# First modulation weights loaded and multiplied by halves of their columns, key-weight chunks loaded between them, one late subtraction, new instruction orders

## The chip, the core and the metric

The kernel runs on one core of a Trainium2 chip. Its five queues are TensorE (PE, with PEld for its weight loads), VectorE (DVE), ScalarE (ACT), GpSimd (POOL) and SyncE (SP), which issues most DMAs. The metric is device time in microseconds of one execution. The kernel before took 1062.74 us, the median of 3 runs (1060.46 to 1064.73).

## What is computed

An adaLN block on 2048 tokens of width D = 576: a linear attention with 32 heads of 18, then an MLP of 4608, both modulated by a condition c. Cut to what matters:

```python
mod = (silu(c) @ w_mod).reshape(1, 6, 1, -1)          # c: (1, 576), w_mod: (576, 3456)
sa, ca, ga, sb, cb, gb = (mod[:, i] for i in range(6))
h = layernorm(x) * (1 + ca) + sa
x = x + ga * attention(h, A_wqkv, A_wo)                # phi(k)^T v, phi(q) kv / (phi(q) z)
h = layernorm(x) * (1 + cb) + sb
return x + gb * (silu(h @ B_w1) @ B_w2)
```

The first thing that the kernel needs is sa and ca: the first 1152 columns of w_mod, multiplied by silu(c).

## The kernel before

**Tiling.** Tokens lie in tiles of 128, four to a block. The width 576 is four chunks of 128 (k = 0 to 3) and a tail of 64 (k = 4, `KC`), stacked twice where a high and a low part are needed. Products in the attention are split into a high part in a reduced f32 and the rest ("hi" and "lo"), so a chunk of a projection is three products.

**The start, in program order.** SP loads x tiles 0 and 1 (L437), the tail rows of w_mod (`tmod`, L468, two loads), the four chunks of w_mod's first 1152 columns (`mods`, L460, 576 KB each), the key weights' chunks (`acc[0]` to `acc[4]`, L404 to L407), x tiles 2 and 3, and the query weights' chunks. VectorE sets `ones` (L552), a 128 x 128 tile, and some small constants; GpSimd makes the identity `ident`. `keep_busy(n)` (L539) puts n matmuls of `ones` by `ones` on TensorE whose result nobody reads. TensorE then transposes c (L560), ScalarE makes silu(c), `sc` (L561). Two layer norms (statistics L347, pow on GpSimd L353) give x tiles 0 and 1, transposed by `turn_tiles` (L531).

**The modulation.** VectorE multiplies `mods[0]` by `sc` (L583) and adds `mods[1]` and `mods[2]` times theirs (L586), each on 1152 columns at once; of `mods[3]` (`last`) it adds the second plane (L593). TensorE sums over partitions with one-column matmuls, `mod_col_of` (L522): for each k one of `mods[0]`'s first plane, one of `last`'s first plane by `sc`, one of the second plane; `tail_cols` (L519) adds the tail rows. `add_cols` (L526) takes the sums out of PSUM as shift and scale. With these, ScalarE (L607) and VectorE (L372, L272) turn each transposed chunk into hT's hi and lo part. The key weights are split on ScalarE (`w_hi`, L477) and VectorE or GpSimd (`w_lo`, L482, L484). `first_k` and `k_part` (L548) are the key projections of x tiles 0 and 1, 56 matmuls. L873 are the projections after that, L1269 the transposes of tiles 2 and 3.

**The end.** The last unit of the MLP (`up_steps` with `last`) makes four values f00, f01, f10, f11 (L1965 to L1971) and splits them into hi and lo operands hp0, hb0, hp1, hb1: "<" is the copy on ScalarE (L2005), ">" the subtraction on VectorE (L2009). `plain_steps` then multiplies them with w2 for eight token tiles (L2065), the first four with hp0 and hb0, the last four with hp1 and hb1, and stores.

**What sets the order.** `arrange` (L262) chains each engine's instructions in the order that `ORDERS` lists by number. Numbers count an engine's instructions in the order in which the program emits them, from `begun`. So each queue is in order, by these lists, and an instruction that waits holds all behind it. TensorE's numbers at the start: 0 to 10 fillers, 11 the transpose of c, 12 to 19 fillers, 20 to 24 `tail_cols`, 25 to 34 `turn_tiles`. VectorE's: 0 `ones`, 1 to 5 small memsets, 6 and 7 the halves of x tile 0's statistics, 9 and 10 those of tile 1. GpSimd's: 0 and 1 the identity, 2 the first pow.

Of the kernel before, what the change touches and what calls it, by code (L numbers as in the profile page):

```python
# [24 lines left out]
def kernel(ctx: ExitStack, tc, A_x, A_wqkv, A_wo, B_x, B_w1, B_w2, c, w_mod, out):  # L25
# [33 lines left out]
    def behind(instructions):  # L59

        with ExitStack() as order:
# [7 lines left out]
            0-24 27-29 25-26 30-44 47 49 51 53 55 57-58 45-46 48 50 59-62 52 54 63-66 69-70 56 73-74 67-68 71-72 75-76  # L69
            79-80 83-84 87-88 77-78 91-92 81-82 85-86 101-102 89-90 95-96 99-100 93-94 103 97-98 106-107 104-105  # L70
            108-123 128-133 136-137 124-127 134 138-139 135 140-163 166-169 164-165 170-187 306 188-191 330 307
            194-201 192-193 202-211 331 212-219 308-309 332-335 220-233 310-311 336-337 234-243 250-255 244-245
            256-265 246-249 312-319 266-267 338-339 278-281 340-343 282-287 344-345 288-295 320-329 268-269 346-347
            270-273 296-297 274-277 354-367 298-301 348-349 368-369 350-351 302-303 352-353 370-381 304-305 382-385
            402-403 386-395 404-409 418-419 410-411 396-397 446-447 420-421 412-417 448-455 398-399 456-457 422-427
            400-401 428-445 458-471 474-475 472-473 476-497 502-507 498-501 508-525 586-591 526-529 610-611 530-533
            592-593 534-535 612-613 536-537 594-595 614-617 538-541 558-561 618-623 542-543 596-597 624-625 598-599
            626-629 562-563 544-549 600-603 564-565 604-607 630-631 550-551 566-569 632-633 608-609 570-573 552-557
            634-641 658-663 642-657 664-665 574-583 666-667 584-585 682-695 668-675 726-727 676-677 728-729 698-701
            696-697 702-703 678-681 704-713 730-731 714-725 732-751 754-757 752-753 758-773 782-787 774-777 788-793  # L80
            778-781 794-803 890-891 804-809 892-893 866-867 894-895 868-869 810-811 870-873 812-815 896-897 816-829
            874-875 898-903 830-843 876-885 904-907 844-851 908-909 886-889 852-855 910-911 856-863 914-917 912-913
            918-919 864-865 920-929 938-951 930-937 1006-1011 952-953 978-979 962-973 1012-1015 954-955 980-997
            1016-1017 998-1005 1018-1035 956-959 1036-1051 1062-1069 974-975 1052-1055 976-977 960-961 1056-1061
            1070-1073 1147-1158 1074-1081 1090-1091 1082-1089 1092-1099 1159 1100-1105 1118-1135 1106-1109 1160-1166
            1136-1139 1110-1111 1140-1141 1167-1170 1112-1113 1142-1143 1114-1117 1144-1145 1207-1222 1197-1200
            1195-1196 1201 1223-1226 1146 1227-1230 1171-1194 1255-1256 1297-1298 1257-1262 1231-1254 1202-1203
            1263-1266 1204-1206 1267-1270 1299-1302 1271 1303-1304 1272-1295 1305-1324 1296 1325-1382 1399-1402
            1383-1386 1427-1428 1403-1408 1429-1434 1387-1392 1435-1440 1393-1398 1409-1414 1441-1444 1415-1422
            1455-1456 1423-1424 1445-1452 1425-1426 1453-1454 1457-1476 1483-1484 1511-1514 1485-1492 1515-1516  # L90
            1477-1482 1493-1496 1517-1534 1497-1504 1535-1538 1505-1510 1539-1552 1567-1568 1553-1558 1595-1596
            1559-1562 1569-1572 1563-1566 1597-1600 1573-1580 1601-1602 1581-1586 1603-1606 1587-1594 1639-1642 1623
            1607-1622 1627 1643-1646 1624-1625 1671-1672 1647-1648 1626 1649-1658 1628 1699-1700 1659-1662 1629
            1673-1674 1630 1663-1666 1675-1676 1631 1701 1632-1633 1635-1637 1634 1702-1710 1638 1711-1714 1677-1680
            1755-1756 1715-1716 1681-1682 1717-1722 1667 1683-1684 1668 1723-1726 1669-1670 1685-1698 1727 1741
# [12 lines left out]
            2138-2140 2157-2160 2141-2142 2161-2164 2175-2178 2165-2174 2183-2185 2193-2194 2203-2204 2195 2186 2205
            2179-2180 2196 2189-2190 2181-2182 2191 2206 2192 2187 2207-2208 2188 2209-2214 2199 2197-2198 2215-2216
            2200-2202 2217-2218 2227 2221-2222 2239 2228-2230 2223-2226 2231 2253 2240 2232-2233 2241-2244 2254-2257  # L110
            2245 2234 2219 2246-2248 2235 2258 2220 2249-2252 2236-2238 2259-2267 2273 2268 2279-2281 2269-2271 2274
            2282 2272 2285 2275-2278 2286-2290 2283-2284 2297 2291 2298-2314 2292-2296 2315-2356 2365-2366 2377
            2357-2358 2378-2381 2359-2362 2367 2382 2371 2363-2364 2389-2390 2368 2372-2374 2369 2375-2376 2370
            2391-2400 2407-2412 2383 2413-2414 2384-2388 2447-2449 2427-2428 2450-2451 2429-2431 2401-2402 2452
            2415-2416 2403 2432 2417 2404 2433 2405 2418 2434 2419-2420 2406 2499 2511-2516 2465-2472 2421-2424 2435
            2485 2500 2425-2426 2436-2439 2486 2440 2487-2491 2441-2442 2492 2443-2444 2501-2504 2445-2446 2453-2458
            2537 2523-2528 2473-2478 2459-2464 2538-2544 2493 2479 2494-2498 2529-2530 2480-2484 2505-2510 2551-2556
            2517-2521 2563-2567 2522 2568-2570 2531-2536 2577-2584 2557-2559 2545-2550 2591-2596 2571-2576 2560
            2603-2604 2561-2562 2605-2608 2597-2599 2585-2587 2600-2602 2588-2590 2615-2621 2609-2612 2623-2624 2622
            2625 2613-2614 2626 2629-2636 2627-2628 2637-2642 2683-2687 2649 2663 2650 2643-2646 2664 2647-2648  # L120
            2651-2654 2688 2655 2665-2668 2656-2662 2669-2675 2689-2690 2677-2679 2676 2680 2691 2681 2692-2695 2682
            2701-2704 2696-2697 2705-2706 2698-2700 2707-2717 2719 2727-2728 2720-2725 2718 2729-2731 2739-2740 2817
            2741-2743 2818 2744-2746 2732-2738 2747-2752 2759-2760 2819-2821 2753-2756 2726 2757 2765-2766 2758
            2761-2762 2767-2770 2763-2764 2771-2776 2785-2787 2835-2836 2777-2778 2837-2838 2805 2779-2781 2839 2782
            2797 2840 2798 2783-2784 2806-2808 2799-2800 2809-2810 2788-2789 2811 2801-2804 2812 2822 2813-2816
            2790-2792 2873-2874 2853 2793 2841 2794-2796 2842-2843 2875-2876 2854-2856 2823-2828 2877-2878 2844 2829
            2879-2880 2845-2846 2830-2833 2857-2859 2847-2848 2834 2893-2897 2849-2850 2861-2865 2860 2866-2867 2898
            2868-2870 2851-2852 2911-2912 2871-2872 2913-2914 2881-2882 2915 2883 2916-2918 2884-2887 2899-2906
            2888-2892 2907-2909 2931-2934 2919-2921 2910 2922-2930
# [472 lines left out]
    for k in START:  # L602
# [7 lines left out]
        if k < KC:  # L610
            first_k(k)
# [1823 lines left out]
```

## Time and profile before

| | |
|---|---|
| median of 3 runs | 1062.74 us |
| the profiled execution | 1062.19 us |
| its span, first to last instruction | 1060.5 us |
| busy: PE, PEld | 1048.6 us (99%), 740.5 us (70%) |
| busy: DVE, ACT, POOL | 867.0 us (82%), 718.5 us (68%), 741.8 us (70%) |
| DMA | 198.75 MB, 187 GB/s over the span |
| granted TensorE clock | 1.00 |

A line of the timeline is: start, length, engine, line of the kernel, operation, the tile written and the tiles read, partitions x elements, count, and in brackets the idle time before it with what ended it. A line of the waits is: who waited for whom, total, times, longest. A window line gives the stretch, its length, the busy time (and instructions) of each engine asked for, the granted clock, the DMA engines' mean busy share and GB/s. Busy TensorE includes the fillers.

### The profile page before, as it was taken

To read this page: it belongs to the slowest core of one execution; us is meant where nothing else is said; L and a number is where in the kernel's file an instruction comes from. 1 tells how busy PE (TensorE), PEld (TensorE's weight loads), DVE (VectorE), ACT (ScalarE), POOL (GpSimd) and SP (SyncE) were. 2 spreads that over 40 slices of the span, in tenths; PEclk is the share of its full clock that TensorE was granted. 3 is DMA by queue.
4 is the path that set the end of the run, shared out by engine and by line. 5 is a ranking of instruction groups with operands and counts; after the bars stand their busy time and mean duration, and the time that the engine had idled before them with its cause. 6 is when DMAs were issued, how large, how long until landed. Compare 5 with 4: busy or idle time off the path is not lost.

```text
span 1060.5 us, 19049 instructions
## 1 busy us (share of the span) xinstructions
PE 1048.6 (99%) x7001; PEld 740.5 (70%) x7001; DVE 867.0 (82%) x1439; ACT 718.5 (68%) x1342; POOL 741.8 (70%) x809
## 2 busy tenths in 40 slices
PE   9999999999999999999999999999999999999998
PEld 9999999887775555666666666666666666666665
DVE  6777675789989898898987888978977977898767
ACT  6875484368667876776865876767757766766554
POOL 3656536566843788899797688876876878787463
PEclk9999999999999999999999999999999999999999
DMA  8596970495657785588478566667567567526422
GB/s 301 159 204 197 155 191 8 104 209 133 185 175 249 241 255 187 179 292 209 125 259 211 175 223 220 172 219 215 183 209 204 185 216 223 187 90 203 152 80 113
DMA packets 139246, 198.75 MB, mean 187 GB/s; under 512 B 63820, under 2 KB 96464, under 8 KB 139152
## 3 DMA queue, kind: packets, MB, share of 16 engines
q1 hardware_dynamic: 106340, 196.35, 61.1%
q10 hardware_dynamic: 32812, 1.18, 3.1%
q8 instruction: 55, 0.90, 0.4%
q14 instruction: 39, 0.32, 0.1%
HBM read 176.77 MB, written 15.48 MB: 181 GB/s over the span
## 4 chain that ended last, share of the span: by engine, by line
PE 92%; DMA 3%; DVE 2%; ACT 1%; SPq 1%; issue 0%; ACTq 0%; DVEq 0%
PE up L1947 33%; PE down L2031 32%; PE psK L873 9%; PE big L400 6%; PE psG L998 5%; PE small L1452 2%; PE big L1463 1%; PE psK L1210 1%; DMA hT<-hd 1%; DMA xt<-in_A_x_dram 1%; PE small L385 1%; DMA acc<-in_A_wqkv_dram 1%; PE down L2065 1%; PE up L2065 1%; PE psG L1171 0%; DMA hd<-S 0%
## 5 line engine op out<-in xcount | busy, mean ns | idle before, releaser
L1947 PE MATMUL up<-hT,w 128*128 128x512 f16 x1264 | 319.2, 379 | 2.2 <-DMA hT<-hd 2.2
L1947 PEld LDWEIGHTS <-w 128*128 128x128 f16 x1492 | 145.7, 98 | 135.3 <-issue 4.6
L2040 DVE SCALAR_TENSOR_TENSOR acc<-acc,set,down 128x576 f32<-128x576 f32 x128 | 103.5, 810 | 34.6 <-PE down L2031 33.6
L1965 ACT ACTIVATE f<-f,set 128x512 f32<-128x512 f32 x102 | 73.3, 719 | 62.6 <-DVE f L1971 52.6
L1985 POOL TENSOR_TENSOR s<-f,f 128x256 f32<-128x256 f32 x66 | 54.4, 825 | 73.3 <-ACT f L1966 70.9
L2031 PE MATMUL down<-w,hc 128*128 128x288 f16 x600 | 91.5, 286 | 0.0
L2031 PE MATMUL down<-w,hb 128*128 128x288 f16 x600 | 90.8, 286 | 0.0
L2031 PE MATMUL down<-w,hT 128*128 128x288 f16 x480 | 82.8, 286 | 0.4 <-DVE acc L2044 0.4
L1969 DVE TENSOR_TENSOR f<-up,p 128x512 f32<-128x512 f32 x102 | 69.5, 683 | 16.4 <-PE up L1947 8.2
L1966 ACT ACTIVATE f<-f,set 128x512 f32<-128x512 f32 x102 | 73.6, 722 | 3.3
L2031 PEld LDWEIGHTS <-hc 128*128 128x128 f16 x600 | 58.7, 98 | 23.1
L2031 PEld LDWEIGHTS <-hb 128*128 128x128 f16 x600 | 58.7, 98 | 22.2 <-issue 0.2
L2009 POOL TENSOR_TENSOR hc<-s,hc 128x512 f16<-128x512 f32 x50 | 63.6, 1272 | 8.2 <-ACT hc L2005 8.2
L1971 DVE TENSOR_TENSOR f<-up,f 128x512 f32<-128x512 f32 x68 | 46.8, 688 | 24.9 <-PE up L1947 24.1
L400 PE MATMUL big<-w,qT 128*128 128x288 f16 x448 | 65.4, 286 | 1.2 <-DMA qT<-w 1.2
L1989 POOL TENSOR_TENSOR f<-f,s 128x256 f32<-128x256 f32 x66 | 53.8, 815 | 18.1 <-DVE hb L2009 10.2
L2031 PEld LDWEIGHTS <-hT 128*128 128x128 f16 x480 | 47.0, 98 | 26.6 <-issue 0.8
L1982 POOL TENSOR_TENSOR s<-f 128x256 f32<-128x256 f32 x66 | 57.3, 869 | 5.6 <-ACT f L1962 4.3
L1987 POOL TENSOR_TENSOR s<-s,f 128x256 f32<-128x256 f32 x66 | 55.9, 847 | 3.5
L2031 PE MATMUL down<-w,ha 128*128 128x288 f16 x396 | 56.6, 286 | 0.0
L2031 PE MATMUL down<-w,hd 128*128 128x288 f16 x396 | 56.0, 286 | 0.0
L2009 POOL TENSOR_TENSOR hd<-s,hd 128x256 f16<-128x256 f32 x66 | 49.0, 742 | 7.0 <-ACT hd L2005 6.9
(424 smaller groups left out, 2767.2 us busy)
## 6 DMA issues: line engine op xcount, KB each, us to landing
hT<-hd SPq DMA_DIRECT2D x101, 640.0 KB, 4.3
hT<-hd SPq DMA_DIRECT2D x65, 512.0 KB, 4.3
hT<-in_B_w_dram SPq DMA_DIRECT2D x14, 576.0 KB, 5.5
hT<-in_B_w_dram SPq DMA_DIRECT2D x28, 256.0 KB, 7.5
raw<-in_B_w_dram SPq DMA_DIRECT2D x11, 576.0 KB, 5.7
v<-in_B_w_dram SPq DMA_DIRECT2D x9, 576.0 KB, 5.1
acc<-in_A_x_dram SPq DMA_DIRECT2D x16, 288.0 KB, 3.5
raw<-in_B_w_dram SPq DMA_DIRECT2D x9, 512.0 KB, 5.7
```

The costliest lines, as they stand in the source:

```text
L400: T.matmul(ps, xpart(a), wpart(b), start=n == 0, stop=n == len(XW) - 1)
L873: T.matmul(o, part(a), w(b), start=c == 0 and m == 0, stop=c == KC and m == 1)
L1947: T.matmul(ps, left, right, start=first and m == 0, stop=m == len(seq) - 1, skip_group_check=True)
L1965: A.activation(f, f, AF.Silu, scale=factor(self.g, "inv"))
L1966: A.activation(f, f, AF.Identity, scale=factor(self.g, "delta"))
L1969: V.tensor_add(f, self.bank[bank[1]], self.p1)
L1982: G.tensor_sub(self.s3, half(i, 0, 0), half(i, 0, 1))
L1985: G.tensor_add(self.s[:, 0:1], half(i, 0, 1), half(i, 1, 1))
L1987: G.tensor_sub(self.s[:, 1:2], self.s[:, 0:1], half(i, 0, 0))
L2009: eng.tensor_sub(t[:, :, 1, :], src, t[:, :, 0, :])
L2031: T.matmul(ps[:, p, :HALF], left[:, u, p * P : (p + 1) * P], right[:, v], start=n in (1, 5, 7, 6) and j == 0, stop=j == len(passes) - 1, s ...
L2040: V.scalar_tensor_tensor(dst, dst, factor(self.g, "ratio"), ps[:, :, :HALF], op0=ALU.mult, op1=ALU.add)
```

## The change

The first 1152 columns of w_mod are loaded and multiplied as two halves of each plane's columns: 0 to 255 (for k = 0 and 1) and 256 to 575 (for k = 2, 3, 4). So there are eight loads instead of four, and eight multiplications on VectorE instead of five; `add_cols` is called four times instead of three. In program order the key chunks 0 and 1 are loaded after the first half, 2 to 4 after the second. `keep_busy` is called with other numbers: ahead of the key projections 2 + 3 + 3 for each half and 1 per k and 1 per half, in place of 4 + 4 + 4, 1 per k, and 2.

```diff
-    def load_mod0():
+    mod_cols = (0, 2 * P, (0, 1)), (2 * P, D, (2, 3, KC))
+
+    def load_mod0(c0, c1):
         for k in range(KC):
             src = w_mod[k * P : (k + 1) * P, 0 : 2 * D].rearrange("p (a d) -> p a d", a=2)
-            nc.sync.dma_start(mods[k][:, :, :D], src)
+            nc.sync.dma_start(mods[k][:, :, c0:c1], src[:, :, c0:c1])
...
-    load_mod0()
-    load_w(0, START)
+    for c0, c1, ks in mod_cols:
+        load_mod0(c0, c1)
+        load_w(0, ks)
...
-    V.tensor_scalar(rows, rows, sc[:, 0:1], None, op0=ALU.mult)
-    keep_busy(4)
-    for k in range(1, KC - 1):
-        V.scalar_tensor_tensor(rows, mods[k][:, :, :D], sc[:, k : k + 1], rows, op0=ALU.mult, op1=ALU.add)
-        keep_busy(4)
...
+    for c0, c1, ks in mod_cols:
+        y = rows[:, :, c0:c1]
+        V.tensor_scalar(y, y, sc[:, 0:1], None, op0=ALU.mult)
+        keep_busy(2)
+        for k in range(1, KC - 1):
+            V.scalar_tensor_tensor(y, mods[k][:, :, c0:c1], sc[:, k : k + 1], y, op0=ALU.mult, op1=ALU.add)
+            keep_busy(3)
+        if KC in ks:
+            A.copy(mods[0][:, 0, D:DX], mods[0][:, 0, KC * P : D])
+        for k in ks:
+            mod_col_of(k, 0, mods[0], ones[:, 0:1])
+            keep_busy(1)
+        V.scalar_tensor_tensor(y[:, 1], last[:, 1, c0:c1], sc[:, KC - 1 : KC], y[:, 1], op0=ALU.mult, op1=ALU.add)
+        if KC in ks:
+            A.copy(last[:, 0, D:DX], last[:, 0, KC * P : D])
+            A.copy(mods[0][:, 1, D:DX], mods[0][:, 1, KC * P : D])
+        for k in ks:
+            mod_col_of(k, 0, last, sc[:, KC - 1 : KC], True)
+            mod_col_of(k, 1, mods[0], ones[:, 0:1], True)
+            if k != 3:
+                add_cols(k - (k == KC), k + 1)
+        keep_busy(1)
+        for k in ks:
+            w_hi(wk_, k, acc[k])
...
```

The splits of the key weights, the chunks of hT and `first_k` stay as they were, inside the loop over halves. The late subtraction:

```diff
-            do("hp0< hp0> hb0< hb0> hp1< hp1> hb1< hb1>")
+            do("hp0< hp0> hb0< hb0> hp1< hp1> hb1<")
...
+        room = room_name(u, "hb", 1)
+        plan.add("DVE", 0.86, lambda: u.step("hb1>"), [source(u, "hb", 1), room + "<", f"U{2 * u.pair + 1}"], [room + ">"])
```

And the lists, of which the beginnings of the new ones matter here. From about the 350th instruction of TensorE and the 90th of VectorE on they are the old lists, renumbered, but for one instruction of TensorE and two of ScalarE in the middle.

```diff
         "PE": """
-            0-24 27-29 25-26 30-44 47 49 51 53 55 57-58 45-46 48 50 59-62 52 54 63-66 69-70 56 73-74 67-68 71-72 75-76
+            0-11 25-26 12-23 29 24 27-28 32-33 43 45 47-48 30-31 34-38 49 39-42 44 46 50-51 68-69 76 78 70-71 80 82-83
+            72-73 84-87 74-75 77 79 81 88 52-55 58-59 62-63 66-67 91-92 95-96 56-57 99-100 60-61 64-65 89-90 93-94
+            97-98 101-102 108-109 112-121 103-104 132-133 110-111 122-123 105-106 124-129 134-139 130-131 142-147 107
         "DVE": """
-            5 0 7 6 9 2 1 3 10 8 11-12 16 13 4 14-15 17-21 24-25 22 38 41-42 39 43 27 23 40 44 28-30 34 32-33 46 49 47
+            7 1 3 5 4 2 0 6 8-12 14-15 13 16-19 53 42-44 20 27-30 21 35 22-23 46 31 45 47-48 25-26 32 40 50 33-34
         "Activation": """
-            1 0 2 4-5 8 6-7 31 3 9 12 10 13 20 30 15 11 14 17 16 21 19 18 25 22 26-27 23 28 24 29 42 48 46 44 47 40 43
+            1 0 2 4-6 9 30 7-8 31 18 3 15 10 13-14 12 11 22 17 16 26 19 28 21 20 23 27 24 29 47 42 25 46 48 43-44 32
         "Pool": """
-            0-3 5 8 6 4 9 71 11 15 10 7 14 13 12 20 16 19 21 23 22 24 26 25 17-18 35 37 36 38-43 27 29 31 33 28 30 32
+            2 0-1 71 8 3 9 6 4-5 11 15 7 14 13 10 19-20 12 16 22 21 23 25 24 26 17-18 35 37 36 38-43 27 29 31 33 28 30
         "SP": """
-            1 0 2-5 13 6-8 12 14 10 15 9 11 18 17 19 16 20 22 21 30-31 34 32-33 24 26 23 25 62 27 40 35 37 28-29 39 41
+            0-2 8 4-5 7 3 6 18 11 15 12 10 13 19 9 20 17 14 16 21 26 22 24 23 25 36 34-35 37 29 27 30 28 38 66 31 44
```

In the new numbers of SP, 0 and 1 are x tiles 0 and 1, 2 and 3 the tail rows, 4 to 7 the first half of w_mod's chunks, 8 and 9 key chunks 0 and 1, 10 to 13 the second half, 14 to 17 the other key chunks, 18 and 19 x tiles 2 and 3, 20 to 25 the query weights, 26 the x rows of the next block. In those of TensorE, 35 to 51 and 68 to 88 are the fillers and modulation columns of the two halves; 52 to 67, 89 to 104 and 108 to 131 are the key projections; 105 to 107 are fillers.

More of the change, by code (lines that the diff above doesn't have):

```diff
@@ L74 @@
[L74 to L83, printed above, removed]
@@ new lines @@
+            856-859 914-915 860-867 918-921 916-917 922-923 868-869 924-933 942-955 934-941 1010-1015 956-957 982-983
+            966-977 1016-1019 958-959 984-1001 1020-1021 1002-1009 1022-1039 960-963 1040-1055 1066-1073 978-979
+            1056-1059 980-981 964-965 1060-1065 1074-1077 1151-1162 1078-1085 1094-1095 1086-1093 1096-1103 1163-1164
+            1104-1109 1122-1139 1110-1113 1165-1170 1140-1143 1114-1115 1144-1145 1171-1174 1116-1117 1146-1147
+            1118-1121 1148-1149 1211-1226 1201-1204 1199-1200 1205 1227-1230 1150 1231-1234 1175-1198 1259-1260
@@ new lines @@
+            1301-1302 1261-1266 1235-1258 1206-1207 1267-1270 1208-1210 1271-1274 1303-1306 1275 1307-1308 1276-1299
+            1309-1328 1300 1329-1386 1403-1406 1387-1390 1431-1432 1407-1412 1433-1438 1391-1396 1439-1444 1397-1402
+            1413-1418 1445-1448 1419-1426 1459-1460 1427-1428 1449-1456 1429-1430 1457-1458 1461-1480 1487-1488
+            1515-1518 1489-1496 1519-1520 1481-1486 1497-1500 1521-1538 1501-1508 1539-1542 1509-1514 1543-1556
+            1571-1572 1557-1562 1599-1600 1563-1566 1573-1576 1567-1570 1601-1604 1577-1584 1605-1606 1585-1590
@@ new lines @@
+            1607-1610 1591-1598 1643-1646 1627 1611-1626 1631 1647-1650 1628-1629 1675-1676 1651-1652 1630 1653-1662
+            1632 1703-1704 1663-1666 1633 1677-1678 1634 1667-1670 1679-1680 1635 1705 1636-1637 1639-1641 1638
+            1706-1714 1642 1715-1718 1681-1684 1759-1760 1719-1720 1685-1686 1721-1726 1671 1687-1688 1672 1727-1730
+            1673-1674 1689-1702 1731 1745 1761-1766 1732-1734 1746 1767-1768 1735 1769-1779 1736-1738 1780-1784
+            1739-1740 1747 1741 1748-1750 1742-1743 1751 1744 1752-1757 1785-1786 1758 1827-1829 1787-1788 1799-1800
@@ new lines @@
+            1830 1801-1806 1789 1807-1812 1831 1843 1790 1844-1846 1813-1818 1832-1833 1847-1848 1819-1820 1791-1792
+            1851 1793-1794 1849 1834 1795 1835 1850 1852-1854 1796-1798 1836-1838 1821-1826 1839 1855-1860 1840-1841
+            1861-1862 1887 1842 1863-1868 1883-1884 1939 1869-1870 1940 1871-1876 1885 1888-1892 1886 1899-1900
+            1877-1878 1893 1879-1880 1901-1902 1941-1942 1903-1908 1943 1909-1910 1953 1894-1895 1881-1882 1944
+            1911-1912 1896-1898 1913-1922 1954 1945 1955 1946-1947 1923-1926 1956-1957 1948 1958 1949-1951 1927-1928
@@ new lines @@
+            2743-2744 2821 2745-2747 2822 2748-2750 2736-2742 2751-2756 2763-2764 2823-2825 2757-2760 2730 2761
+            2769-2770 2762 2765-2766 2771-2774 2767-2768 2775-2780 2789-2791 2839-2840 2781-2782 2841-2842 2809
+            2783-2785 2843 2786 2801 2844 2802 2787-2788 2810-2812 2803-2804 2813-2814 2792-2793 2815 2805-2808 2816
+            2826 2817-2820 2794-2796 2877-2878 2857 2797 2845 2798-2800 2846-2847 2879-2880 2858-2860 2827-2832
+            2881-2882 2848 2833 2883-2884 2849-2850 2834-2837 2861-2863 2851-2852 2838 2897-2901 2853-2854 2865-2869
@@ new lines @@
+            306 308 329 323 330-331 296 314-316 108 317-318 298 339-341 319 332 324-326 351-352 309 342 353 363 327
+            364-365 333 335 354 334 336 345 299 374 338 337 328 375-376 366 355 346 372 356 347 357 348 358-359
+            343-344 360 377 350 385-387 349 373 407-408 300 409 361 367 369 362 382 388 384 371 378 391 368 383 379
+            434-435 389 380 400 390 392 397 436 393 370 410 381 398 401 394 413-416 437 395-396 417 423 404 424
+            443-444 405 422 418 421 406 445 425 438-439 399 442 420 411 446 426 514 419 427 402 429 431 412 403
@@ L156 @@
+            577 576 568 572 583 622 575 578 574 569 581-582 584 586 580 579 589 566 592 595 598 593 587 597 600-601
+            599 607 588 606 590-591 609-610 594 604 614 596 611 617 615 602 605 619 621 608 635-637 625 624 626-627
+            641-642 616 643 645 628 603 612 629 631 633 632 623 630 650 613 618 639 634 660 652 638 640 655 647 649
+            656 658 648 651 659 654 653 657 646 644
         """,
         "Activation": """
[L158 removed]
@@ new lines @@
+            32 34 45-46 44 48 47 49-51 76 52 58 61 53 60 54 62-63 56 64 67 59 65 55 66 68-70 73 72 74-75 77 80 57
+            78-79 81-83 86 84-85 87-88 90 93 91-92 89 94-95 97 100 98-99 103 101-102 96 104-106 110 107-108 111-112
+            114-117 109 130 118-119 131-132 120-121 142 134 122 124-125 113 158 126-127 135-136 123 128 137 133
+            138-139 129 147 157 148-150 140-141 143-146 151 160 162-164 159 196 161 197 178 180 165 152 166-167 181
+            169 155 168 170 172 175 177 171 198 173 202 182 176 174 183-184 199 156 187 185 188 206 190 189 191 179
@@ L197 @@
+            178 161 155 159 164 160 162-163 175 168 165 180 177 166 188 187 169 167 171 176 172 197 196 173 182 174
+            184 201 181 186 189 205 185 190-192 198 211 183 199 195 200 202-204 206 208 213 212 216 193 217 209 207
+            214 220 194 215 218-219 210
         """,
@@ L582 @@
     rows, last = mods[0][:, :, :D], mods[KC - 1]
-    V.tensor_scalar(rows, rows, sc[:, 0:1], None, op0=ALU.mult)
-    keep_busy(4)
-    for k in range(1, KC - 1):
-        V.scalar_tensor_tensor(rows, mods[k][:, :, :D], sc[:, k : k + 1], rows, op0=ALU.mult, op1=ALU.add)
-        keep_busy(4)
-    A.copy(mods[0][:, 0, D:DX], mods[0][:, 0, KC * P : D])
-    for k in START:
-        mod_col_of(k, 0, mods[0], ones[:, 0:1])
-        keep_busy(1)
-    for c0, c1 in ((0, 2 * P), (2 * P, D)):
-        V.scalar_tensor_tensor(rows[:, 1, c0:c1], last[:, 1, c0:c1], sc[:, KC - 1 : KC], rows[:, 1, c0:c1], op0=ALU.mult, op1=ALU.add)
@@ L594 @@
-    A.copy(last[:, 0, D:DX], last[:, 0, KC * P : D])
-    A.copy(mods[0][:, 1, D:DX], mods[0][:, 1, KC * P : D])
-    for k0, k1 in ((0, 1), (1, 3), (3, KC + 1)):
-        for k in range(k0, k1):
+    for c0, c1, ks in mod_cols:
[15 more added lines that the diff above has]
+        for k in ks:
@@ L598 @@
             mod_col_of(k, 0, last, sc[:, KC - 1 : KC], True)
             mod_col_of(k, 1, mods[0], ones[:, 0:1], True)
-        add_cols(k0, k1)
-    keep_busy(2)
-    for k in START:
-        w_hi(wk_, k, acc[k])
-        w_lo(wk_, k, acc[k], V if k in (1, 3) else G)
-        pt, _, to, col, h = args[k]
-        hi, lo = (k, KC + k) if k < KC else (2 * KC, 2 * KC + 1)
-        A.activation(to[:, hi, :], pt, AF.Identity, bias=col[:, k, 0:1], scale=col[:, k, 1:2])
-        modulate(*args[k], V)
-        sub_hi(to[:, lo, :], h, to[:, hi, :])
-        if k < KC:
-            first_k(k)
+            if k != 3:
+                add_cols(k - (k == KC), k + 1)
@@ L612 @@
+        keep_busy(1)
+        for k in ks:
+            w_hi(wk_, k, acc[k])
+            w_lo(wk_, k, acc[k], V if k in (1, 3) else G)
+            pt, _, to, col, h = args[k]
+            hi, lo = (k, KC + k) if k < KC else (2 * KC, 2 * KC + 1)
+            A.activation(to[:, hi, :], pt, AF.Identity, bias=col[:, k, 0:1], scale=col[:, k, 1:2])
+            modulate(*args[k], V)
+            sub_hi(to[:, lo, :], h, to[:, hi, :])
+            if k < KC:
+                first_k(k)
     keep_busy(3)
```

146 lines of the change are left out of this document (56 added, 90 removed).

## Prediction

> **What bounds the kernel now.** I read the share of each engine first, then TensorE's waits, then the chain that ended last.
>
> ```profile
> span 1060.5 us, 19049 instructions
> PE 1048.6 (99%) x7001; PEld 740.5 (70%) x7001; DVE 867.0 (82%) x1439; ACT 718.5 (68%) x1342; POOL 741.8 (70%) x809
> ...
> PE up L1947 <- DMA hT<-hd: 2.2, 1, 2.2
> PE psG L542 <- DVE ones L552: 1.2, 1, 1.2
> ...
> PE down L2065 <- ACT hc L2005: 0.5, 1, 0.5
> ...
> PE down L2031 <- DVE acc L2044: 0.4, 1, 0.4
> ```
>
> TensorE is busy for 1048.6 of 1060.5 us. A change wins only by removing one of its few idle spans, or by removing work from its queue; it loses whatever it puts into that queue, or whatever it starts late. The edit touches the two ends, so the next view is TensorE's busy time by stretch (columns: stretch, its length, busy time, instructions, granted clock, DMA share, GB/s).
>
> ```profile
> 0.00:30.00 30.00, 27.88 (x209) 1.00 0.86 292
> 30.00:320.00 290.00, 288.40 (x2148) 1.00 0.67 155
> 320.00:360.00 40.00, 36.10 (x204) 1.00 0.77 249
> 360.00:1039.00 679.00, 678.99 (x4319) 1.00 0.63 196
> 1039.00:1046.00 7.00, 6.02 (x41) 1.00 0.00 0
> ```
>
> In the first 30 us TensorE is idle for 2.12 us, around 1039 to 1046 for 0.98 us. So even a perfect change has little to win there: at the start 2.12 us less the 1.15 us before the first instruction, about 1.0 us. "Busy" at the start does not mean useful, though: much of it is `keep_busy`, matmuls of ones that only occupy the array. They are in the same in-order queue as the work. TensorE's queue by time:
>
> ```profile
> 1.15 4.96 PE L542 MATMUL psG<-ones 128*128 128x128 f32 x22 [1.15 <-DVE ones L552]
> 6.04 0.22 PE L560 MATMUL psG<-ident,crow 5*128 5x5 f32 x1
> ...
> 13.71 1.28 PE L522 MATMUL psG<-ones,hT 128*128 128x1 f32 x10
> ...
> 18.45 0.51 PE L548 MATMUL psK<-w,hT 128*128 128x288 f32 x2
> ...
> 28.59 0.51 PE L873 MATMUL psK<-wq,hT 128*128 128x288 f32 x2
> ```
>
> An f32 matmul stands as two passes (11 fillers are x22), a transpose as one. Key projections (L548) start at 18.45, the next projections (L873) at 28.59, and from there the queue is full. Two stretches between, of all TensorE instructions:
>
> ```profile
> 13.71:18.45 4.74, 4.74 (x43) 1.00 1.04 377
> 18.45:28.59 10.14, 10.01 (x79) 1.00 0.77 264
> ```
>
> From 13.71 to 18.45 the queue runs without a gap: 42 passes (the 43rd straddles the end) in 4.74 us, 0.113 us each, though most are one-column matmuls or fillers. So before 18.45 the price of the start is already a count of passes.
>
> **The change, part by part.**
>
> *The first order of VectorE.* Its list now begins 7 1 3 5 4 2 0. Number 0 is the memset of `ones`, which every filler reads; number 7 is the second half of the statistics of x tile 0.
>
> ```profile
> 0.93 0.17 DVE L552 MEMSET ones<- 128x128 f32 x1
> 4.54 1.58 DVE L347 BATCH_NORM_STATS2 st<-xt 128x6 f32<-128x288 f32 x4 [3.44 <-DMA xt<-in_A_x_dram]
> 5.67 0.06 DVE L554 MEMSET neghalf<- 128x4 f32 x1
> 5.00:10.00 5.00, 4.33 (x33) 4.03 (x32) 3.17 (x15) 1.52 (x6) 0.71 (x1) 1.00 1.01 345
> ...
> xt<-in_A_x_dram SPq DMA_DIRECT2D x4, 288.0 KB, 6.9
> ```
>
> Before, `ones` was ready at 1.10 and TensorE began at 1.15. Now VectorE's queue stands still until x tile 0 lands. Before, tile 0 was the second load and released VectorE at 4.54; now it is the first, with 288 KB fewer ahead of it, 0.85 us at the 345 GB/s of the windows' row: 3.7, as an estimate. Then 0.40 for number 7 (1.58/4), at most 5 x 0.06 for the memsets and 0.17 for `ones`: 4.55. Fillers start at 4.5 instead of 1.15, with bounds of 4.2 (memsets all overlapped) and 5.4 (no earlier landing). Queued behind the waiting instruction are all of VectorE, so the fillers, so the transpose of c (number 11 on TensorE, behind the 11 fillers), so silu(c), and with it the multiplication of every w_mod chunk.
>
> *The eleven first fillers.* 22 passes take 4.96 us, 0.225 each, twice the later price. The fillers' own rows show when that ends:
>
> ```profile
> 5.00:5.50 0.50, 0.50 (x4) 0.50 (x4) 1.00 0.73 263
> ...
> 7.00:7.50 0.50, 0.50 (x7) 0.50 (x6) 1.00 1.02 364
> ```
>
> Four passes in half a microsecond at 5.0, seven at 7.0, the granted clock reading 1.00 in both. The array was thus slow for some 5.8 us from its first instruction. I keep 4.96 for the block, wherever it begins: it ends at 4.5 + 4.96 = 9.5, the transpose at 9.7 (0.22), against 6.26 before. Bounds: 22 x 0.113 = 2.5 us if it were fast at once; 0.9 us more (8 passes at 0.113 extra) if the slow time lasts 5.8 us from the new start, to 10.3. The Trainium skill ("TensorE: Matmul & The Clock Gate", Part 1) says that the array runs at half rate until about 3.4 us of sustained activity, in a free-running window. By that rule 15 passes would be slow and 7 fast, 4.2 us, and the sum below would be 0.8 us smaller; the trace's 5.8 us is longer than one window and fits a first window that was only partly busy. I go by the trace.
>
> GpSimd's list now begins with the pow of the first layer norm (2) and makes the identity after it (0, 1), which the transpose of c needs.
>
> ```profile
> 0.80 0.20 POOL masks.py:197 MEMSET ident<- 128x128 f32 x1 [0.29 <-POOLq L2421]
> 1.08 0.29 POOL masks.py:199 TENSOR_SCALAR_AFFINE_SELECT ident<-ident 128x128 f32<-128x128 f32 x1
> 6.65 0.71 POOL L353 TENSOR_TENSOR mv<-mv,neghalf 128x2 f32<-128x2 f32 x1 [5.28 <-DVE mv L352]
> ```
>
> The pow would run at about 6.3 to 7.0 and the identity be ready at 7.5: hidden behind the fillers' 9.5, but a floor of 7.5 if they ran fast.
>
> *The passes between.* I counted them in the new order. Up to the first key projection there were 121 passes: 70 of fillers, 30 of modulation columns, 10 of tail columns, 10 transposes, 1 for c. `keep_busy` now adds 11 + 8 + 11 + 12 calls ahead of it, 84 passes: 135 in all, 112 of them after the transpose of c. All of the second half's columns (76 to 88) still stand ahead of the first projection (52). So the two halves do not let the projections begin early: the list has them wait for both. 112 x 0.113 = 12.7 us; start of L548 at 9.7 + 12.7 = 22.4, against 18.45.
>
> Is anything else late there? VectorE: silu is ready some 0.2 after the transpose, at 9.9; one half of the four instructions is about 0.4 + 2 x 0.7 + 0.5, from these rows.
>
> ```profile
> 8.33 0.82 DVE L583 TENSOR_SCALAR hT<-hT,sc 128x1152 f32<-128x1152 f32 x1 [1.76 <-DMA hT<-in_w_mod_dram]
> ...
> 12.24 1.42 DVE L586 SCALAR_TENSOR_TENSOR hT<-hT,sc 128x1152 f32<-128x1152 f32 x1 [0.40 <-DMA hT<-in_w_mod_dram]
> 13.91 0.95 DVE L593 SCALAR_TENSOR_TENSOR hT<-hT,sc 128x256 f32<-128x256 f32 x2 [0.25 <-DMA hT<-in_w_mod_dram]
> ```
>
> So the first half is done by 12.4, the first columns reach TensorE's turn near 13. Loads: the last w_mod transfer of the old list, with 3312 KB issued up to it, released L593 at 13.91. The new list has x tile 2 and key chunks 0 and 3 ahead of it (288 KB each) and half of chunk 4 (144 KB) no longer: 4032 KB, 720 KB more, 2.1 us at 345 GB/s, so 16.0. TensorE asks for it near 20. The loads are hidden with 4 us to spare; shorter rows may cost some of that. The four issues more on SP (0.55 each by the pairs below) hide as well, since SP waits for landings anyway; the query weights' chunks 2 to 4, now behind a 1152 KB load of x, land near 27, for use after 31.
>
> ```profile
> 2.96 1.10 SPq L460 DMA_DIRECT2D hT<-in_w_mod_dram x2
> ```
>
> ScalarE holds `act` of chunk 0 behind the copy of the last columns (10 behind 15), some 18 us; its first reader is now at 22.4. Both covers are gone if TensorE were on time.
>
> *From the first projection on.* The fillers there fall from 12 passes to 4 before L873 begins:
>
> ```profile
> 18.45:28.59 10.14, 1.98 (x12) 1.72 (x12) 1.00 0.77 264
> ```
>
> 8 x 0.113 = 0.9 us less. L873 then starts at 22.4 + 10.1 - 0.9 = 31.6, that is 3.0 us later than 28.59. The cover for everything else there is VectorE's lead:
>
> ```profile
> 20.00:40.00 20.00, 19.86 (x152) 19.52 (x151) 19.44 (x47) 18.78 (x35) 8.80 (x10) 1.00 0.55 174
> ```
>
> It is full (third busy time, 19.44 of 20), and TensorE did not wait for it. By a walk along its new list with these durations it falls back by about 2 us, TensorE by 3, so the lead grows; if it did not, each microsecond of VectorE's lag would come on top.
>
> *Does the delay reach the end?* The chain of waits between:
>
> ```profile
> 29.21 6.39 PE psK L873 x48
> ...
> 326.23 4.88 DMA hd<-S
> ...
> 346.73 8.88 DMA hT<-hd
> ```
>
> The transfers on which TensorE waits at 320 to 360 hang on VectorE and TensorE work just before them in the chain, not on a clock of their own. I let all of the 3.0 us through.
>
> *The late subtraction.* The list of the last unit no longer holds hb1>; it is planned in `plain_steps` behind U's last addition.
>
> ```profile
> 1039.93 1.84 DVE L2009 TENSOR_TENSOR hb<-f,hb 128x512 f16<-128x512 f32 x1
> 1041.69 0.80 DVE L2040 SCALAR_TENSOR_TENSOR acc<-acc,set,down 128x576 f32<-128x576 f32 x1
> 1042.42 0.68 DVE L1969 TENSOR_TENSOR f<-up,p 128x512 f32<-128x512 f32 x1
> ```
>
> The 1.84 us leave the path from f01 to f10. L1969 needs its matmuls, over at 1041.7, so it moves up by 0.7, and the two stalls of 0.37 and 0.55 shrink. The 4 us that follow have room for hb1>, whose reader comes four tiles later. I take -0.5, bounds -0.9 and 0.
>
> **Sum.** +3.0 - 0.5 = +2.5 us. The profiled execution is 1062.19 us (span 1060.5 and 1.7 around it), so 1064.7; the median of the three runs, 1062.74, gives **1065.2**. Bounds of the start: lowest is the identity's floor, 7.5 + 0.2 + 12.7 + 9.2 - 28.6 = +1.0; highest +3.0, 0.9 for the later landing, 0.9 for slow passes: +4.8.
>
> **Rivals.** (1) *The halves do what they say:* chunks 0 and 1 are modulated while the second half lands, TensorE is never short. This needs fillers that do not hold the queue. The start can win the 1.0 us of idle above at most, less 14 passes (1.6) plus 8 (0.9), and the tail 0.5 to 0.9: 1061.5. Against it: 42 passes without a gap. Chance 0.12. (2) *The delay is given back* at 320 to 360, where 3.9 us are idle, if the transfers there are paced by DMA: 1062.7 - 0.5 = 1062.2. The chain speaks against it. 0.13. (3) *The array stays slow:* the block starts later, pauses for silu and columns come in between, and the slow rate lasts past 10.3 for half of the trace's 5.8 us again: 2.9/0.225 = 13 passes x 0.112 = 1.5 us, on top of +4.8 - 0.5: 1062.7 + 5.8 = 1068.5. It decides if the fillers still take 0.225 at 12 us. For it: 5.8 us slow before, without a pause. Against it: after 7.0 no pause of the old list brought the slow rate back. 0.2. Forecast: 0.55, with 1063.2 to 1067.0 of its own.
>
> **How the numbers follow.** Range 1061.5 to 1069.0: rivals 1 and 2 at its lower end, the most of rival 3 within. About 0.5% (5.3 us, 1057.4 to 1068.1) is what a measurement of this kernel can tell from no change. Slower by more: most of rival 3, 0.13. Faster by more would need 5.3 us where 1.0 and 0.9 are idle: 0.03. Same: 0.84.
>
> **What would show it.** Right: TensorE's first filler near 4.5, released by `ones`; transpose of c near 9.7; first L548 near 22.4; first L873 near 31.6; no idle time between; L2065 0.5 us sooner after the last L1947. Wrong: fillers at 0.113 from the start, L548 before 20, or a wait on DVE or DMA after L873 has begun.

## The result: 0.7% slower

The changed kernel took 1070.84 us (median of 14 runs, 1069.75 to 1075.17), the kernel before 1063.86 us (14 runs, 1059.75 to 1069.07): ratio 1.0073, interval 1.0058 to 1.0089. Lines behind the start have other numbers in the changed kernel: +3 near the start (L545 fillers, L551 first key projections), +5 and +6 later (L680 is the old L674, L879 the old L873).

### The profile page after: what moved, and what is told of

The parts are those of the page before. It is cut to its first block, busy times and chain, and to the rows that moved or that the text cites. A ratio compares the mean times of both kernels' runs of the same rounds, so it can differ in the third digit from the quotient of the medians.

```text
span 1068.9 us, 19072 instructions
## 1 busy us (share of the span) xinstructions
PE 1052.8 (98%) x7009; PEld 744.2 (70%) x7009; DVE 873.8 (82%) x1443; ACT 717.4 (67%) x1342; POOL 743.9 (70%) x809
## 4 chain that ended last, share of the span: by engine, by line
PE 91%; DMA 4%; DVE 3%; ACT 1%; issue 1%; SPq 0%; POOL 0%; ACTq 0%; DVEq 0%; POOLq 0%
PE up L1953 33%; PE down L2037 31%; PE psK L879 9%; PE big L400 5%; PE psG L1004 5%; PE small L1458 2%; DMA acc<-in_A_wqkv_dram 1%; PE big L1469 1%; DMA hT<-hd 1%; PE small L385 1%; PE psK L551 1%; PE down L2071 1%; DMA qT<-pn 1%; PE up L2071 1%; PE psK L1216 0%
```

## The profile after

The changed kernel's page, span and busy time, and then TensorE's waits (total, times, longest):

```profile
span 1068.9 us, 19072 instructions
...
PE 1052.8 (98%) x7009; PEld 744.2 (70%) x7009; DVE 873.8 (82%) x1443; ACT 717.4 (67%) x1342; POOL 743.9 (70%) x809
```

```profile
PE psG L545 <- DVE ones L555: 4.7, 1, 4.7
PE small L385 <- ACT H L370: 3.8, 1, 3.8
PE psG L525 <- DVE col_a L529: 0.8, 1, 0.8
...
PE down L2071 <- DVE U L2050: 0.4, 1, 0.4
```

The first wait was foreseen (4.5). The second was not, and it is neither at the start nor at the end. TensorE is also busy for 4.2 us longer than before (1052.8 against 1048.6), with 8 instructions more: some of its work ran slower. Its queue at the start:

```profile
4.65 4.33 PE L545 MATMUL psG<-ones 128*128 128x128 f32 x22 [4.65 <-DVE ones L555]
8.91 0.22 PE L563 MATMUL psG<-ident,crow 5*128 5x5 f32 x1
...
18.54 0.61 PE L525 MATMUL psG<-ones,hT 128*128 128x1 f32 x4 [0.80 <-DVE col_a L529]
...
21.59 2.81 PE L545 MATMUL psG<-ones 128*128 128x128 f32 x12
24.05 5.51 PE L551 MATMUL psK<-w,hT 128*128 128x288 f32 x36
...
33.38 0.96 PE L879 MATMUL psK<-wq,hT 128*128 128x288 f32 x6
```

Fillers at 4.65 (forecast 4.5), transpose of c at 8.91 (9.7), key projections at 24.05 (22.4), L879 at 33.38 (31.6; before 28.59). Two things make the late part later than forecast: a wait of 0.80 us, and twelve filler passes (six fillers) that take 2.46 us from their start to that of the next group, 0.205 each, where 0.113 was the price. The windows say why (fifth column: granted clock):

```profile
0.00:30.00 30.00, 24.54 (x176) 0.94 0.90 293
21.70:25.10 3.40, 3.40 (x17) 0.50 1.04 342
...
247.00:250.40 3.40, 0.59 (x5) 1.00 0.31 127
250.40:253.80 3.40, 2.38 (x11) 0.50 0.35 81
253.80:257.20 3.40, 3.40 (x16) 0.50 0.15 18
320.00:360.00 40.00, 39.21 (x239) 1.00 0.71 241
```

Three stretches of 3.41 us ran at half clock, two of them behind a hole at 247 to 250. In the hole ScalarE stands, and SP and TensorE around it (three timelines, one engine each):

```profile
241.88 1.05 ACT L680 ACTIVATE w<-w 128x1024 f32<-128x1024 f32 x1
242.82 0.20 ACT L680 ACTIVATION_READ_ACCUMULATOR w<-w 128x1 f32 x1
248.82 1.16 ACT L680 ACTIVATE w<-w 128x1152 f32<-128x1152 f32 x1 [5.80 <-DMA w<-in_B_w_dram]
```

```profile
242.86 1.79 SPq L1386 DMA_TRANSPOSE qT<-pn  x1
244.74 0.52 SPq L679 DMA_DIRECT2D w<-in_B_w_dram  x1
```

```profile
251.43 0.47 PE L385 MATMUL small<-ident,xn 128*128 128x128 f32 x1 [3.83 <-ACT H L370]
```

The same place in the kernel before:

```profile
236.93 1.05 ACT L674 ACTIVATE w<-w 128x1024 f32<-128x1024 f32 x1
237.88 0.20 ACT L674 ACTIVATION_READ_ACCUMULATOR w<-w 128x1 f32 x1
237.97 1.16 ACT L674 ACTIVATE w<-w 128x1152 f32<-128x1152 f32 x1
```

L680 squares pieces of B's weights and sums them. Before, the wide square stood right behind the 1024 one. Now it waits 5.80 us for its data, because of the exchange of two instructions that "The change" mentions ("two of ScalarE in the middle") and the forecast's sum does not:

```diff
-            221 219 237 227-228 224 236 262 249 231 233 232 229 234 263 238 212 240 239 248 241-242 244-245 264 243
+            221 219 237 227-228 224 236 248-249 231 233 232 229 234 263 238 212 240 239 262 241-242 244-245 264 243
```

Number 262 reads a piece that had been loaded already. Number 248 reads the room that 236, the 1024 square just ahead of it, must free first. That square is done at about 243.0; SP is then in a DMA transpose until 244.65, issues the load at 244.74, and the load lands some 4 us later. So of the 5.80 us some 1.7 are SP's queue and 4 the load. ScalarE is in order, so H (L370) and, behind H, TensorE's transposes wait too.

Comparing the start times of the same TensorE instruction in both traces, the changed kernel is 4.9 us late at 75, 11.8 at 246, 9.0 from 420 on and 8.3 at the end. So the start costs nearly 5 in this execution (the half-clock stretch at 21.7 included), the hole and the slow stretches behind it 7, 3 come back between 320 and 360, and 0.65 is won at the tail. The one instruction of TensorE that the lists also move in the middle, near 160 us, leaves no mark: 4.9 us late at 150, 4.8 at 200.

## The experiments

The theory: most of the loss is the exchange of the two squares; the start costs what its later fillers and its passes cost. The rivals: the whole start is the fault of `ones`; the halves themselves cost; half clock costs by itself. Each ratio is against the kernel before on the same chip.

**The exchange alone**, in the kernel before: its ScalarE list with "236 248-249 … 262" as above, nothing else.

> The kernel before, with only the two instructions of ScalarE exchanged that the new list exchanges in the middle: two squares of the weight scan, of which the one now earlier reads a room that the square just ahead of it has to free first. Theory (the exchange makes the stall at 247 to 251 us of the changed kernel): ScalarE waits some 5.8 us for the load there, TensorE 3.8 us, TensorE's slow rate follows for some 6.8 us, and of the 6 us lost some 2 come back at 320 to 360; 1.003 to 1.005 of the kernel before. Rival (the load was late because everything was late after the start): no stall, 1.000.

Measured: 1069.24 us, ratio 1.0055 (1.0036 to 1.0075), 5.9 us of 1063.81, a little more than the theory's 1.005. TensorE waits the same 3.8 us in the same place:

```profile
PE small L385 <- ACT H L370: 3.8, 1, 3.8
```

**The changed kernel without the exchange**: the two numbers put back.

> The changed kernel with these two squares in their old order. Theory: no wait of TensorE on L370 near 240 to 252, the delay of the start (4.9 us at 200) stays and loses up to 2.2 us at 320 to 360: 2.3 to 4.9 us above the kernel before, 1.002 to 1.005. Rival: stall still there, 1.007.

Measured: 1066.93 us, ratio 1.0022 (1.0008 to 1.0035): 2.3 us. Together the two are 8.2 us of a loss of 7.0 (medians) to 7.8 (ratio). The exchange is the larger part, shown from both sides; start and tail cost 2.3 us by the ratio (0.9 to 3.7 by its interval), and the forecast had said 2.5.

**The late subtraction alone**, in the kernel before:

```diff
-            do("hp0< hp0> hb0< hb0> hp1< hp1> hb1< hb1>")
+            do("hp0< hp0> hb0< hb0> hp1< hp1> hb1<")
...
+        plan.add("DVE", 0.86, lambda: u.step("hb1>"), [source(u, "hb", 1), room + "<", f"U{2 * u.pair + 1}"], [room + ">"])
```

> The kernel before with the late subtraction alone. Theory: the 0.4 and 0.5 us for which TensorE waits between 1043 and 1046 shrink by 0.4 to 0.5 us together; 0.9995. Rival (it takes the time elsewhere at the end): 1.000 or above.

Measured: 1064.05 us, ratio 0.9999 (0.9983 to 1.0015). In its trace TensorE gains 0.65 us on the kernel before between 1040 and 1045, as in the changed kernel's; the time does not resolve it.

**`ones` late, alone**, in the kernel before:

```diff
-            5 0 7 6 9 2 1 3 10 8 11-12 16 13 4 14-15 17-21 24-25 22 38 41-42 39 43 27 23 40 44 28-30 34 32-33 46 49 47
+            5 7 0 6 9 2 1 3 10 8 11-12 16 13 4 14-15 17-21 24-25 22 38 41-42 39 43 27 23 40 44 28-30 34 32-33 46 49 47
```

> The kernel before with ones made only after the first statistics of x tile 0, nothing else. Theory (passes behind ones): first filler near 4.5, transpose of c near 9.7, first key projection 2.5 us later than 18.45; 1.002. Rival (w_mod's loads hide it, since VectorE waits for them up to 13.9 anyway): 18.5 as before, 1.000.

Measured: 1066.04 us, ratio 1.0025 (1.0008 to 1.0043).

```profile
5.24 4.44 PE L542 MATMUL psG<-ones 128*128 128x128 f32 x22 [5.24 <-DVE ones L552]
9.60 0.22 PE L560 MATMUL psG<-ident,crow 5*128 5x5 f32 x1
...
21.01 0.51 PE L548 MATMUL psK<-w,hT 128*128 128x288 f32 x2
...
30.75 0.51 PE L873 MATMUL psK<-wq,hT 128*128 128x288 f32 x2
```

Fillers 4.1 us later, key projections 2.6, L873 2.2. So late fillers delay the end though their result is read by nobody.

**`ones` first in the changed kernel**, with the identity first on GpSimd; once with the exchange and once without:

```diff
-            7 1 3 5 4 2 0 6 8-12 14-15 13 16-19 53 42-44 20 27-30 21 35 22-23 46 31 45 47-48 25-26 32 40 50 33-34
+            0 7 1 3 5 4 2 6 8-12 14-15 13 16-19 53 42-44 20 27-30 21 35 22-23 46 31 45 47-48 25-26 32 40 50 33-34
```

> The changed kernel with ones made first on VectorE and the identity first on GpSimd. Theory (the start is a count of TensorE passes behind ones): first filler near 1.2, transpose of c near 6.1, first key projection at 18.8 to 20 instead of 24.05, L879 at 28.5 to 30 instead of 33.4; the stall near 247 stays: 1.003 to 1.005. Rival (the halves and their later loads make the start late): first key projection still at 22 or later, 1.006 or more.

> Both repairs. Theory: within 1 us of the kernel before, 0.999 to 1.001, since the halves by themselves neither cost nor win much, and the late subtraction wins 0.3 to 0.5 us at the end. Rival (something else in the orders costs): 1.002 or more.

Measured: 1072.51 us, ratio 1.0082 (1.0065 to 1.0099), and 1066.45 us, 1.0023 (1.0009 to 1.0037). No gain: the theory that `ones` alone makes the start late falls. The rival's sign, a first key projection at 22 or later, is there (25.47 in the first of the two), but what its TensorE shows first is a pause that no load ends:

```profile
5.96 0.22 PE L563 MATMUL psG<-ident,crow 5*128 5x5 f32 x1
8.24 0.44 PE L534 MATMUL psK<-ident,xt 128*128 128x128 f32 x2 [2.05 <-DVE xt L364]
```

c is transposed 2.95 us sooner, and then TensorE stands 2.05 us before a transpose of x that the new list puts early, and runs three stretches at half clock behind that (9.2 to 19.4). I then tried to take the pauses away one after the other.

**The transposes of x behind more fillers** (on the version with `ones` first and without the exchange, ScalarE's list adapted), and then, on top, six fillers fewer:

```diff
-            0-11 25-26 12-23 29 24 27-28 32-33 43 45 47-48 30-31 34-38 49 39-42 44 46 50-51 68-69 76 78 70-71 80 82-83
+            0-19 25-26 29 20-24 27-28 32-33 30-31 34-38 43 45 47-48 49 39-42 44 46 50-51 68-69 76 78 70-71 80 82-83
```

> The changed kernel with the two squares back, ones and the identity first, and on TensorE the first fillers ahead of the transposes of x tile 0, so that the queue does not stand for the layer norm; on ScalarE the normalisation of tile 1 ahead of the cast of key chunk 0. Theory: no wait of 2 us near 6 to 8, no slow array after it, first key projection near 19 to 20, L879 near 28.5 to 29.5; 0.999 to 1.0005. Rival (the halves themselves, their loads or the 14 further passes, make the start late): first key projection at 21 or later, 1.002.

> The same with six fillers fewer ahead of the key projections (12 passes). Theory of passes: 1.4 us sooner than the run with them. Rival (the fillers keep the array fast: with so many one-column matmuls the rate halves and the projections themselves run slow): no sooner, or later by up to 1.7 us for each stretch of 3.4 us at half clock.

Measured: 1068.84 us, 1.0041 (1.0023 to 1.0059), and 1069.2 us, 1.0052 (1.0035 to 1.007). Both theories fail. In the first, the pause moved on, to the columns that read the tail rows of w_mod, and brought half clock again (the profile names no releaser, "issue"; the next experiment shows that it was the rows):

```profile
11.12 2.08 PE L522 MATMUL psG<-z,tmod 128*128 128x2 f32 x10 [2.24 <-issue]
```

In the second, the projections begin sooner (22.36, in the first 26.54) and run slower: 36 passes take 7.72 us, where at full clock (L551 of the last experiment) they take 5.28.

```profile
22.36 7.72 PE L551 MATMUL psK<-w,hT 128*128 128x288 f32 x36
```

**Both tail rows loaded early**, on top of the transposes of x behind more fillers:

```diff
-            0-2 8 4-5 7 3 6 18 11 15 12 10 13 19 9 20 17 14 16 21 26 22 24 23 25 36 34-35 37 29 27 30 28 38 66 31 44
+            0-5 7 6 8 18 11 15 12 10 13 19 9 20 17 14 16 21 26 22 24 23 25 36 34-35 37 29 27 30 28 38 66 31 44
```

> The kernel with the squares back, `ones` first and the transposes of x behind more fillers, and now both tail rows of w_mod (SP's numbers 2 and 3) among the first loads, where the one before had the second of them behind x tile 2's and found TensorE standing 2.24 us before a tail column. Theory that the halves themselves are free and that all of the start's loss comes from pauses early in TensorE's queue, each with a stretch at half clock behind it: no pause of over 0.5 us before 20 us, no window at clock 0.50 behind 8 us, first L551 at 19 to 20.5, ratio 0.9985 to 1.0005. Rival, that the 14 passes more ahead of the key projections and the loads in halves cost by themselves (or that another late load takes the pause): first L551 at 21 or later, ratio 1.002 or more.

Measured: 1068.68 us, 1.0048 (1.0033 to 1.0064): the rival's side. That pause is gone; the next one (2.06 us before one of the first half's columns, released by VectorE) has taken its place. Its windows, one row per stretch:

```profile
11.80:15.20 3.40, 1.34 (x12) 1.00 1.06 399
15.30:18.70 3.40, 3.21 (x17) 0.50 1.07 318
18.70:22.10 3.40, 3.40 (x29) 1.00 1.03 310
22.10:25.50 3.40, 3.40 (x18) 0.50 1.05 338
```

The first drop follows a pause. The second follows a stretch in which TensorE was busy all the time; what stood there were mostly one-column matmuls (the second half's columns). That gave the next theory.

**Six fillers fewer in the kernel before** (12 of its passes): of the calls of 4, 4, 4 the last becomes 2, and of five single ones between the columns one stays.

> The kernel before with six fillers (12 passes) fewer between the modulation columns, nothing else. Theory of the pass count: the first L548 comes 12 x 0.113 = 1.4 us sooner if the modulation is ready by then, ratio 0.9987. Rival, that the fillers keep the array at full clock while VectorE makes the modulation: TensorE waits for VectorE instead, L548 comes less than 0.5 us sooner, and a window at clock 0.50 follows within 10 us; ratio 1.000 to 1.003.

Measured: 1064.33 us, 1.0007 (0.999 to 1.0024). No gain, as the rival said; whether there is a loss the interval leaves open. In its profile, the first drop comes behind a pause (2.37 us, for the normalised x) that the kernel before has as well in some executions (2.9 us in the trace of the exchange alone, whose start is that of before); a second, at 19.9, comes behind a stretch with 0.25 us of idle time and few wide passes. The first:

```profile
9.60:13.00 3.40, 1.03 (x9) 1.00 1.03 363
13.00:16.40 3.40, 3.40 (x19) 0.50 1.06 326
```

**Narrow fillers in the kernel before**: 19 of its fillers one column wide.

```diff
-            T.matmul(kvp[2][:, 1, P : 2 * P], ones, ones, start=True, stop=True, skip_group_check=True)
+            T.matmul(kvp[2][:, 1, P : P + m], ones, ones[:, :m], start=True, stop=True, skip_group_check=True)
...
-    keep_busy(4)
+    keep_busy(4, 1)
```

> The kernel before with the 19 fillers between and behind the modulation columns made one column wide instead of 128; number, order and everything else unchanged (their result is read by nobody). In the trace of before a one-column pass took the same 0.113 us as a filler, so the queue is as long and as free of gaps as it was. Theory (wide work rule), from the stretches of 3.41 us in the ten traces so far: the array runs the next stretch at half clock when fewer than about 11 passes of 128 columns, of the 30 that fit, stood in this one, whether it stood idle or did one-column passes. Then the stretch from 13.7 to 18.5, now nearly all narrow, brings one or two stretches at clock 0.50 in nearly every execution: mean clock of the runs 0.9965 or less (before: 0.998), ratio 1.0015 to 1.004. Rival (only standing idle lowers the clock): clock as before, 0.998, ratio 0.999 to 1.001.

Measured: 1070.67 us, 1.0066 (1.0045 to 1.0086); mean clock of the runs 0.991 (of the kernel before, beside them, 0.9987). The theory holds, by more than it said. TensorE is never short of work, and four stretches run at half clock:

```profile
10.20:13.60 3.40, 3.38 (x32) 1.00 1.05 396
13.60:17.00 3.40, 3.40 (x18) 0.50 1.04 352
17.00:20.40 3.40, 3.40 (x17) 0.50 1.04 402
20.40:23.80 3.40, 3.40 (x17) 0.50 1.05 359
23.80:27.30 3.50, 3.50 (x16) 0.51 0.29 88
27.30:30.70 3.40, 3.40 (x29) 1.00 0.15 20
```

**The last six fillers between the columns**, in the changed kernel without the exchange:

```diff
-            0-11 25-26 12-23 29 24 27-28 32-33 43 45 47-48 30-31 34-38 49 39-42 44 46 50-51 68-69 76 78 70-71 80 82-83
-            72-73 84-87 74-75 77 79 81 88 52-55 58-59 62-63 66-67 91-92 95-96 56-57 99-100 60-61 64-65 89-90 93-94
+            0-11 25-26 12-23 29 24 27-28 32-33 43 45 47-48 30-31 34-38 49 39-42 44 46 50-51 68-69 76 70 78 71 80 72 82 73
+            83 74-75 84 77 85 79 86 81 87 88 52-55 58-59 62-63 66-67 91-92 95-96 56-57 99-100 60-61 64-65 89-90 93-94
```

> The changed kernel with the old order of the two squares, and the last six fillers of the second half (12 passes behind its last columns) put between its columns; no pass more or less. Wide work rule: the stretch of 18 narrow passes that the profile showed ahead of a drop to 0.50 now holds 20 wide ones as well, so that drop is gone: mean clock 0.999 or more (without the move 0.9984), ratio 1.0015 to 1.002; the price of the later start stays, 2.3 us. Rival (narrow passes do no harm): no change of the clock, ratio 1.002 to 1.0025; or the columns, now later by some passes, hold up VectorE and the first L551 comes later than 21.

Measured: mean clock 0.9996 (0.9984 without the move), as the theory said; 1065.35 us, ratio 1.0023 (1.001 to 1.0036), above the theory's 1.0015 to 1.002 and no better than without the move (1.0022). The clock was mended and a gain in time is not shown: the median fell by 1.6 us, but that of the kernel before was lower as well beside these runs (1063.05 against 1063.81). Its TensorE, at clock 1.00 over all the start:

```profile
4.44 4.88 PE L545 MATMUL psG<-ones 128*128 128x128 f32 x22 [4.44 <-DVE ones L555]
9.25 0.22 PE L563 MATMUL psG<-ident,crow 5*128 5x5 f32 x1
...
18.86 0.38 PE L525 MATMUL psG<-ones,hT 128*128 128x1 f32 x2 [0.80 <-DVE col_a L529]
...
23.13 5.28 PE L551 MATMUL psK<-w,hT 128*128 128x288 f32 x36
...
32.45 0.96 PE L879 MATMUL psK<-wq,hT 128*128 128x288 f32 x6
```

Its nine runs at mean clock 1.000 average 1065.3 us, those of the kernel before at 1.000 beside them (9) 1062.1: without any half clock the changed start still costs 3.2 us, the gain of the tail already taken off. No version that I ran beat the kernel before.

## Why the prediction was wrong

It forecast the direction (slower) but 1065.2 us, and its range ended at 1069.0, below the measured 1070.84.

- **The step that failed** is "The edit touches the two ends". It came from reading the diff by its meaning. The lists in the middle also differ, in two ScalarE numbers, and the sum had no term for them. That term is 5.9 us by the first experiment, more than twice the forecast loss. In the changed kernel's trace it is 5.80 us of waiting on ScalarE, 3.83 us of waiting on TensorE, and two stretches at half clock behind that, less what comes back between 320 and 360. The lists and the trace of before could have given most of it: 248 reads a room that 236 frees, and a load of some 4 us lies between.
- **First order of VectorE**: right. Fillers at 4.65 for 4.5; a late `ones` alone, in the kernel before, costs 2.7 us by the ratio (0.9 to 4.6).
- **Eleven first fillers**: 4.33 us for 4.96, c at 8.91 for 9.7. By the Trainium skill's rule ("TensorE: Matmul & The Clock Gate", Part 1; a warm-up of about 3.4 us in a free-running window), the estimate was 4.2 us, nearer than mine here. Over all traces the block takes 4.25 to 5.06 us, so neither is exact. The 5.8 us of slow rate were also too long: the records of the clock begin, at full clock, at 5.88 us in the trace of before and at 8.06 in the changed kernel's, 4.7 and 3.4 us behind the first filler. The passes ahead of these points are 0.213 us apart, the fillers behind them 0.112.
- **112 passes, 12.7 us**: right in price. At clock 1.00 (last experiment) it is 13.66 us from the end of c's transpose (9.47) to 23.13, of which 0.80 is a wait: 12.86.
- **"The loads are hidden with 4 us to spare"**: right of the loads, but not of what comes behind them. The second half's product ended at 18.41, and TensorE waited 0.80 us for an addition of column sums (L529, number 21) that stands behind this product (27 to 30) in VectorE's list. I had taken 0.4 + 1.4 + 0.5 = 2.3 us for one half on VectorE; the second half took 3.8:

```profile
14.53 1.45 DVE L588 TENSOR_SCALAR hT<-hT,sc 128x640 f32<-128x640 f32 x1 [0.34 <-DMA hT<-in_w_mod_dram]
16.02 1.80 DVE L591 SCALAR_TENSOR_TENSOR hT<-hT,sc 128x640 f32<-128x640 f32 x2
17.86 0.55 DVE L598 SCALAR_TENSOR_TENSOR hT<-hT,sc 128x320 f32<-128x320 f32 x1
18.33 0.15 DVE L529 TENSOR_TENSOR col_a<-psG,plus 128x2 f32<-128x2 f32 x1
```

- **"All of the 3.0 us through"**: so for a delay of that size (the last experiment is 4.0 us late at 75 and 4.3 at 345), not for a larger one (the changed kernel falls from 11.8 to 9.0 over 320 to 360, where TensorE's wait for hT, 2.2 us before, is now 0.2).
- **Late subtraction, -0.5**: right in the trace (-0.65), too small to be measured.
- **The rivals**: the first falls, since late fillers do hold the queue (`ones` late, alone); the second in the main, since a delay of 4 us reached the end. The array was slow again, as the third said, but not from its start-up: it went slow again at 21.7, which that rival's own argument against it (no pause of the old list brought the slow rate back) had made unlikely. The old list was mostly spared because wide fillers stood between its columns (made narrow, they brought half clock); the second half's columns have few between them.

Not settled: how much of the start's 2.3 us in the changed kernel falls to the halves and how much to `ones`. With `ones` first, each order I tried without the exchange ran into a pause or into half clock (1.0023 to 1.0052).

## What to carry to other kernels

Compare the instruction lists as lists, to the last number, and follow each exchange to the room it reads and the load behind it: on an in-order engine a reader put directly behind the instruction that frees its room waits for a whole load (here 5.80 us), and so does everything behind it. Fillers on TensorE are work with a purpose: count wide passes per 3.4 us, not busy time, before taking some away or grouping narrow matmuls. And judge a change of a few microseconds by runs of equal mean clock beside the medians; by both, since a change can move the clock itself, as the narrow fillers did.

## What the hardware showed that I had not expected

**Half clock comes in whole stretches of 3.413 us**: the traces record 3.41, 6.83, 10.24 and 13.65 us. That is the free-running window that the Trainium skill names ("TensorE: Matmul & The Clock Gate", Part 1, 3413 ns), and the traces agree on its length. They do not agree with its condition for half clock, at least one idle window: pauses of 1.2 to 2.9 us, shorter than a window, were enough, and so was a stretch without any pause.

**What decides is the wide work in a stretch.** A stretch holds 30 f32 passes of 128 columns (3.413/0.113). I laid the grid of each execution by its first drop, and counted, in 72 stretches from 5 to about 30 us of 11 traces, the time of matmuls of 64 columns or more, as such passes. Of 22 stretches with 10 or fewer, all 22 were followed by half clock; of 44 with 12 or more, none; of 6 with 11, four. Twelve of the 22 had 0.3 us of idle time or less, most of them stretches already at half clock. Such a stretch obeys the same number: at 0.225 us a pass it holds 15, so it gets out by being nearly full of wide work. The stretches outside this count agree: over all 14 traces from end to end, some 4300 stretches, none with 12 or more passes was followed by half clock, and all with 10.8 or fewer were. Idle time alone does not sort them: in the trace of before the stretch at 354 us had 1.6 us of it and 16 passes, and full clock followed; with both tail rows early the stretch at 18.7 had none and 10.8 passes, and half clock followed. The narrow fillers were the test of this, and it held; that it is the count of columns, and not something that goes with it, was not tried further.

**It goes with about half of the spread of the kernel before.** One stretch of 3.41 us at half clock loses 1.7 us, 0.0016 of the span in the mean clock. The 94 runs of this kernel beside the experiments: at mean clock 1.000 (34 runs) 1062.0 us on average, at 0.999 (5) 1061.8, at 0.998 (24) 1063.9, at 0.997 (18) 1064.5, at 0.996 (4) 1064.4, at 0.995 (9) 1066.5. A straight line through them takes up 0.53 of the variance. The changed kernel had no run above 0.998; there, five runs average 1070.6, 6.7 us more than the kernel before at that clock.
